# An H3 convolution mixer and a token MLP on one core: where ssm_D is added, how the filter is cut, and a new order of the work

## The chip, the core and the metric

The kernel runs on one core of one Trainium2 chip. A core has five engines with a queue of instructions each: TensorE (PE, matmuls into PSUM), VectorE (DVE), ScalarE (ACT), GpSimd (POOL) and SyncE (SP, which here only starts DMAs). Every engine works through its queue in order and waits on semaphores. DMAs started by SP, ACT or POOL move data between HBM and SBUF, and also between partitions of SBUF. The metric is the device time of one execution in microseconds, the median of the runs shown.

## The reference

With S = 2048 positions, D = 448 channels and F = 1792:

```python
k_shift = sum over t of k_pad[:, t:t+S, :] * shift_k[:, ks-1-t]      # 4 taps
kv      = k_shift * v
y       = irfft(rfft(kv, 2S) * rfft(ssm_k, 2S))[:S]                  # causal convolution per channel
y       = y + kv * ssm_D
h       = x + layernorm(x) * y                                       # x is A_q
# token MLP on the normalised h, along S:
u  = gelu(einsum("bsd,sf->bdf", layernorm(layernorm(h)), w1) + b1)
h2 = h + transpose(einsum("bdf,fs->bds", u, w2) + b2)
```

The kernel computes h as x + (x - mean) * rstd * y. Since y + kv * D is a convolution with a filter whose tap at position 0 has D added, ssm_D can be put into the filter: in the frequency domain it is one constant added to the real parts of the filter's spectrum.

## The kernel before, in words

S is split as 2048 = 128 partitions x 16 rows (r). The convolution is a Fourier transform of length 4096 in two stages of matmuls against sine tables, for the filter k and for the signal u = kv:

- **Loads** (L855 to L880). SP loads the filter ssm_k (448 x 2048) in chunks of 128, 128, 128 and 64 channels, the taps, k, v, ssm_D and the biases.
- **Tables** (L740 to L840). POOL makes indices, DVE phases and ACT sines, in two halves; table E serves the first stage, FW the second, ET (E transposed by PE, the `ct` step, L1035) the last inverse stage.
- **kT** (L962). PE transposes the filter into KT, 64 transposes into eight PSUM banks; ACT or DVE copies each out (the helper `evac`, L698 to L705). Matmuls of constants (L952) lie in between; nobody reads their result.
- **kv** (L915 to L935). Four matmuls with a column of ones spread the four tap rows over 128 partitions. Then DVE multiplies k by the taps (L926), PE sums the four products with the identity as weights (L932), and DVE multiplies the sum by v out of PSUM (L935), in eight steps.
- **First forward stage** of k and of u (`emit_stage1`, L985): for each of four groups i and four jh, eight matmuls of 128 x 32 weights, an evacuation of 896 columns (L997), and, after every second one, a shuffle between partitions by three DMAs (L1002; two from POOL, one from SP).
- **Second forward stage** (`k2` and `u2`, L1021): 16 evacuations each.
- **Products and first inverse stage** (`i1`): DVE multiplies the two spectra (L1054, 16 times), PE transforms (L1066), ACT or DVE evacuates 16 times, and DMAs shuffle the result to TZ (L1090, the last ones L1079).
- **Second inverse stage** (`i2`, L1157): two matmuls per row r; ACT or DVE multiplies by rstd of x and adds 1 (L1164, L1166); DVE multiplies with x - mean (L1171) and normalises over D (L1177 to L1212), POOL making the powers -0.5 (L1130 for x, L1206 for h). The statistics of x come from DVE (L1122, L1124) and POOL (L1127). Matmuls that nobody reads (L1100, "warm") fill PE until the shuffle has landed and between the first rows.
- **MLP**: first layer (L1257 and L1267, 14 groups of 16 accumulating matmuls), gelu on ACT (L1247), second layer (L1277, 16 rows of 14 matmuls), bias and h added by DVE (L1281), output by SP.

No loop in the program sets the order. Each step is recorded as an operation with its reads and writes; `_Sched.schedule` then plays the whole list with estimated costs (`est`) and lets each free engine take the ready operation with the smallest due number. Those numbers are the table `WHEN`, one per step; `WHERE` says for each evacuation that may go to either engine whether it goes to ACT ("a"), to DVE ("d") or to whichever is free ("f"). The order so planned is emitted as the queues, with waits on semaphores where an operation needs another engine's result. So a change of these two tables moves work on all five queues. PSUM holds four pairs of banks, the shuffle ring four groups.

ssm_D enters in the first forward stage of k: for the matmuls of row r = 0 a second matmul with one row of weights (L990, K = 1) adds DR to the sum in PSUM:

```python
dl = tag == "k" and r == 0
op("pe", ... E[:, 2 * r + x, c0:c0 + 32], src[:, r, :], start=True, stop=not dl ...)
if dl:
    op("pe", ... E[0:1, x, c0:c0 + 32], DR[0:1, :], start=False, stop=True ...)
```

Of the kernel before, what the change touches and what calls it, by code (L numbers as in the profile page):

```python
# [7 lines left out]
ALU = mybir.AluOpType  # L8
# [4 lines left out]
    "dummy": (60,),  # L13
    "tables": (47, 16, 57, 90, 51, 55, 62, 200,),
    "loads": (107, 109, 110, 113, 92, 114, 181, 186, 182, 117, 183, 180, 112,),
    "kv": (0, 152, 118, 19, 40, 142, 157, 143, 161,),
    "kT": (189, 78, 21, 33, 268, 73, 150, 8, 160, 83, 132, 72, 108, 122, 100, 95, 70, 53, 129, 46, 91, 115, 65, 48,
        41, 99, 97, 15, 240, 22, 185, 77, 23, 88, 52, 131, 18, 106, 199, 4,),
    "k1": (98, 104, 145, 140, 32, 76, 124, 154, 79, 1, 134, 159, 102, 141, 147, 156,),
    "k2": (166, 165, 120, 105, 168, 167, 146, 148, 170, 169, 178, 176, 171, 172, 184, 179,),  # L20
    "u1": (28, 38, 82, 162, 39, 96, 119, 144, 11, 26, 43, 128, 5, 49, 66, 138,),
    "xload": (6, 264, 256, 195,),
    "ct": (269,),
    "bias": (29,),
    "q": (273, 271, 272, 263, 260, 262, 275, 266, 265,),
    "u2": (69, 68, 17, 10, 103, 116, 50, 42, 121, 123, 80, 126, 125, 151, 133, 127,),
    "i1": (270, 163, 139, 149, 71, 155, 9, 137, 158, 174, 12, 94, 173, 27, 136, 135,),
    "w1a": (67, 75, 85, 87,),
    "w1b": (35,),
    "warm": (64, 56, 254, 274, 250, 247, 255, 130, 81, 164, 30, 252, 241, 20, 249, 235, 7, 37, 25, 89, 101, 251, 267,  # L30
        93, 257, 259, 253, 258, 208, 246, 86, 111, 276, 177,),
    "i2": (61, 13, 14, 175, 44, 45, 34, 187, 192, 3, 31, 188, 204, 245, 63, 203, 243, 194, 244, 205, 74, 190, 24, 84,
        237, 2, 193, 36, 54, 196, 191,),
    "w2": (153,),
    "mlp": (238, 216, 207, 242, 215, 261, 219, 222, 232, 210, 236, 59, 230, 211, 202, 198, 212, 206, 197, 224, 209,
        221, 218, 220, 214, 201, 233, 231, 226, 225, 217, 223, 227, 239, 228, 234, 213, 58, 229, 248,),
}
WHERE = {
    "kv": "fffa",
    "kT": "fdffdffd",  # L40
    "k2": "ddadfafaaddafffa",
    "ct": "ddaa",
    "bias": "f",
    "u2": "afffffaaafaaafdf",
    "i1": "dadffaaffaafafda",
    "i2": "aaaadffaaffadaff",
# [69 lines left out]
class _Buf:  # L116
    __slots__ = ("pool", "k", "users", "writers", "readers", "slots", "left", "rel")

    def __init__(self, pool, k=1):
        self.pool = pool  # L120
        self.k = k
        self.users = []
        self.writers = []
        self.readers = []
        self.slots = None
        self.left = 0
        self.rel = 0.0


class _Op:  # L130
    __slots__ = ("id", "engs", "eng", "fn", "preds", "spreds", "est", "lat", "is_dma", "nbytes", "keng", "ev",
                 "t0", "rate", "acq", "bufs", "tag", "extra")


class _Sched:
# [51 lines left out]
    def op(self, W, fn, r=(), w=(), br=(), bw=(), n=0, kind=None, est=None, dmab=None, keng=16, rate=None, after=(), safter=()):  # L187
# [3 lines left out]
        o = _Op()  # L191
# [14 lines left out]
        o.ev = None  # L206
        o.t0 = WHEN[self.tag][self.count[self.tag]]
# [88 lines left out]
    def schedule(self):  # L296
# [33 lines left out]
        fab = 0.0  # L330
        events = []
# [34 lines left out]
        while done < n:  # L366
            progressed = False
            for e in ENGS:
                if free_at[e] <= t + 1e-9 and ready[e]:
# [21 lines left out]
                    for b in o.acq:  # L391
                        p = b.pool
                        b.slots = pick(p, b.k)
                        for i in b.slots:
                            o.extra.extend(p.prev[i])
                            p.free_t[i] = INF
                    start[cand] = t
                    free_at[e] = t + o.est[e]
                    if o.is_dma:
# [157 lines left out]
def _build(nc, A_q, A_k, A_v, A_shift_k, A_ssm_k, A_ssm_D, B_w1, B_b1, B_w2, B_b2, out):  # L557
# [55 lines left out]
    with ctx:  # L613
# [63 lines left out]
        def Pb(b, i=0):  # L677
            return PS[:, b.slots[i], 0:D]
# [170 lines left out]
        CW = (128, 128, 128, 64)  # L849

# [486 lines left out]
```

## Time and profile before

| | us |
|---|---|
| median of 5 runs | 187.42 (186.85 to 188.64) |
| the profiled execution | 187.61 |
| its span in the profile | 185.7 |
| PE busy | 177.1 |
| PE weight loads busy | 92.9 |
| DVE busy | 109.4 |
| ACT busy | 95.1 |
| POOL busy | 61.5 |

The granted clock of TensorE is 1.0 in the whole span. Busy times are sums over the span, and a matmul's end is modelled, so a busy PE is not one at its peak. Duration and pace differ: instructions that follow one another overlap a little, so five copies listed at 916 ns each can take less than five times that. In lists by group, the columns are line, engine, operation, out<-in, the shape, the count, then busy us and mean ns of one, then the idle time of the engine ahead of them with what ended it. PEld is the loading of weights.

### The profile page before, as it was taken

To read this page: it belongs to the slowest core of one execution; us is meant where nothing else is said; L and a number is where in the kernel's file an instruction comes from. 1 tells how busy PE (TensorE), PEld (TensorE's weight loads), DVE (VectorE), ACT (ScalarE), POOL (GpSimd) and SP (SyncE) were. 2 spreads that over 40 slices of the span, in tenths; PEclk is the share of its full clock that TensorE was granted. 3 is DMA by queue.
4 is the path that set the end of the run, shared out by engine and by line. 5 is a ranking of instruction groups with operands and counts; after the bars stand their busy time and mean duration, and the time that the engine had idled before them with its cause. 6 is when DMAs were issued, how large, how long until landed. Compare 5 with 4: busy or idle time off the path is not lost.

```text
span 185.7 us, 3193 instructions
## 1 busy us (share of the span) xinstructions
PE 177.1 (95%) x1231; PEld 92.9 (50%) x1231; DVE 109.4 (59%) x182; ACT 95.1 (51%) x138; POOL 61.5 (33%) x153
## 2 busy tenths in 40 slices
PE   7999999999888899999999899999999999999993
PEld 2475333333232333544544344556555577777772
DVE  7968788985779999979998674100000034312221
ACT  3577988896999999951785464412222200000000
POOL 8541519556410055358588764000000000000000
DMA  4999626649649957758999999200000002110022
GB/s 120 408 382 352 219 85 240 231 186 315 223 117 340 399 159 202 215 191 264 397 404 407 422 423 415 110 0 4 0 0 0 0 4 99 49 49 25 0 102 74
DMA packets 14869, 35.44 MB, mean 191 GB/s; under 512 B 3133, under 2 KB 8782, under 8 KB 14854
## 3 DMA queue, kind: packets, MB, share of 16 engines
q1 hardware_dynamic: 11734, 28.41, 41.1%
q0 software_dynamic: 3072, 6.80, 11.6%
q8 instruction: 10, 0.16, 0.4%
q14 instruction: 5, 0.04, 0.1%
q10 hardware_dynamic: 48, 0.03, 0.1%
HBM read 22.37 MB, written 1.84 MB: 130 GB/s over the span
## 4 chain that ended last, share of the span: by engine, by line
PE 83%; ACT 11%; POOL 3%; issue 1%; DVE 1%
PE ps L1277 23%; PE ps L1267 11%; PE ps L1257 8%; PE ps L932 7%; PE ps L985 7%; PE ps L1066 6%; PE ps L1100 5%; ACT arena L701 5%; PE ps L962 3%; PE ps L1157 3%; PE ps L952 3%; ACT arena L997 3%; ACT arena L702 3%; PE ps L1021 2%; PE ps L1035 1%
## 5 line engine op out<-in xcount | busy, mean ns | idle before, releaser
L1281 DVE SCALAR_TENSOR_TENSOR arena<-ps,arena 128x448 bf16<-128x448 f32 x16 | 10.9, 684 | 55.9 <-PE ps L1277 55.9
L1277 PE MATMUL ps<-arena 128*128 128x448 bf16 x224 | 43.8, 353 | 0.0
L1277 PEld LDWEIGHTS ps<-arena 128*128 128x128 bf16 x224 | 32.0, 144 | 11.0 <-ACT arena L1247 1.2
L997 ACT CAST arena<-ps 128x896 bf16<-128x896 f32 x32 | 27.2, 916 | 6.1 <-PE ps L985 6.0
L701 ACT CAST arena<-ps 128x896 bf16<-128x896 f32 (+2 forms) x30 | 23.2, 845 | 5.3 <-PE ps L915 2.8
L1257 PE MATMUL ps<-arena 128*128 128x448 bf16 x112 | 24.4, 353 | 0.4 <-DVE arena L1212 0.4
L1002 POOL DMA_DIRECT2D arena<-arena x32 | 17.7, 558 | 20.4 <-ACT arena L997 20.4
L1267 PE MATMUL ps<-arena 128*128 128x448 bf16 x112 | 22.7, 352 | 0.0
L1247 ACT ACTIVATE arena<-ps,arena 128x448 bf16<-128x448 f32 x14 | 8.5, 634 | 25.1 <-PE ps L1267 21.1
L926 DVE TENSOR_TENSOR arena<-arena 128x1792 bf16<-128x1792 bf16 x16 | 17.1, 1101 | 2.2 <-PE ps L932 2.2
L985 PE MATMUL ps<-arena 128*32 128x448 bf16 x256 | 17.0, 356 | 0.8 <-ACT arena L997 0.4
L1021 PE MATMUL ps<-arena 128*64 128x448 bf16 x128 | 15.8, 361 | 2.0 <-ACT arena L701 1.1
L1054 DVE TENSOR_TENSOR arena<-arena 128x1792 bf16<-128x1792 bf16 x16 | 16.7, 1086 | 0.2
L1257 PEld LDWEIGHTS ps<-arena 128*128 128x128 bf16 x112 | 10.8, 98 | 11.3 <-DVE arena L1212 1.8
L1267 PEld LDWEIGHTS ps<-arena 128*128 128x128 bf16 x112 | 10.9, 98 | 9.9 <-ACT arena L1247 0.2
L1164 ACT ACTIVATE arena<-ps,arena 128x448 f32<-128x448 f32 x14 | 9.8, 722 | 11.1 <-PE ps L1157 7.3
L1090 POOL DMA_DIRECT2D arena<-arena x14 | 8.2, 589 | 20.2 <-ACT arena L701 18.1
L1066 PE MATMUL ps<-arena 64*128 64x448 bf16 x128 | 14.1, 351 | 0.6 <-ACT arena L701 0.5
L932 PE MATMUL ps<-arena 128*128 128x448 bf16 x64 | 14.0, 354 | 0.0
L1171 DVE SCALAR_TENSOR_TENSOR arena<-arena 128x448 f32<-128x448 bf16 x16 | 10.7, 677 | 1.6 <-ACT arena L1164 1.6
L1021 PEld LDWEIGHTS ps<-arena 128*64 128x64 f16 x128 | 5.3, 108 | 12.1 <-ACT arena L701 4.7
L985 PEld LDWEIGHTS ps<-arena 128*32 128x32 f16 x256 | 5.5, 95 | 10.0 <-issue 3.3
(87 smaller groups left out, 196.8 us busy)
## 6 DMA issues: line engine op xcount, KB each, us to landing
arena<-in_B_w_dram SPq DMA_DIRECT2D x8, 896.0 KB, 8.5
arena<-in_B_w_dram SPq DMA_DIRECT2D x2, 2048.0 KB, 16.2
arena<-arena SPq DMA_DIRECT2D x16, 224.0 KB, 2.7
arena<-arena POOLq DMA_DIRECT2D x32, 112.0 KB, 2.9
arena<-in_B_w_dram SPq DMA_DIRECT2D x2, 1536.0 KB, 20.9
arena<-arena POOLq DMA_DIRECT2D x14, 196.0 KB, 4.4
arena<-in_A_k_dram SPq DMA_DIRECT2D x4, 448.0 KB, 7.3
arena<-in_A_v_dram SPq DMA_DIRECT2D x4, 448.0 KB, 8.0
```

Of the source, the lines that this page charges most:

```text
L701: return e.copy(out=dst(), in_=src())
L926: op("dve", lambda e, W, T=T, i=i, r=r: e.tensor_tensor(out=T[:, i], in0=KH[:, r:r + 4, :], in1=WT, op=ALU.mult), r=[(o_KH + r * DB, 4 * D ...
L932: op("pe", lambda e, W, b=b, T=T, i=i, j=j: e.matmul(Pb(b, i), ID, T[:, i, j, :], start=(j == 0), stop=(j == 3)), r=[(o_ID, 256), (o + (i ...
L985: op("pe", lambda e, W, b=b, r=r, q=q, x=x, c0=c0, dl=dl: e.matmul(PS[32 * q:32 * q + 32, b.slots[x], 0:D], E[:, 2 * r + x, c0:c0 + 32], s ...
L997: return e.copy(out=dst, in_=Ppair(b)) if W == "act" else e.tensor_copy(out=dst, in_=Ppair(b))
L1002: shuf[tag].append(op(q_, lambda e, W, g=g, i=i, a=a, nu=nu, jh=jh: e.dma_start(T[a + i:a + i + 4 * nu - 3:4].rearrange("p (j k) c d -> p ...
L1021: op("pe", lambda e, W, b=bs[h], h=h, j=j, c=c, par=par: e.matmul(PS[64 * par:64 * par + 64, b.slots[c], 0:D], FW[:, 64 * c:64 * c + 64], ...
L1054: op("dve", lambda e, W, m=m, i=i: e.tensor_tensor(out=MR(m.slots[0]).rearrange("p (x y) d -> p x y d", x=2), in0=TU[:, i].unsqueeze(2).br ...
L1066: k = op("pe", lambda e, W, b=bs[h], m=ms[h], par=par, t=t, tab=tab, xy=xy, P=P: e.matmul(Pb(b, par), tab[P, :], MR(m.slots[0])[P, xy, :], ...
L1257: op("pe", lambda e, W, r=r, fc=fc, b=bs[fc]: e.matmul(Pb(b), W1A[:, r, 128 * fc:128 * fc + 128], Q[:, r, :], start=(r == 0), stop=(r == R ...
L1267: op("pe", lambda e, W, r=r, fc=fc, b=b: e.matmul(Pb(b), W1B[:, r, 128 * (fc - n0):128 * (fc - n0) + 128], Q[:, r, :], start=(r == 0), sto ...
L1277: op("pe", lambda e, W, r=r, fc=fc, b=b: e.matmul(Pb(b), W2[fc // 7][:, fc % 7, r:S:R], G[:, fc, :], start=(fc == 0), stop=(fc == NFC - 1) ...
```

## The change

It has five parts.

1. ssm_D is no longer added by L990. DR holds it on 16 partitions, with the other partitions zeroed by POOL, and the four evacuations of k's first group (i = 0) become additions of DR on DVE. The other first-stage evacuations, which only ACT did, may go to ACT or DVE.
2. The filter is loaded and transposed in four chunks of 112 channels.
3. The tap rows are spread by matmuls over all 128 partitions (ONE and SK whole), for which DVE zeroes SK before the load of the taps.
4. `WHEN` and `WHERE` are new throughout, so the order on every queue is.
5. The planner's costs change: 100 ns when PE changes the shape of its tiles (`mode`), other estimates for some POOL and PE operations. Every operation on a buffer, not only the first, now waits for the readers of the buffer's previous owner.

The numbers of the lines in the changed kernel are some 8 to 10 higher.

```diff
@@ planner
                         for i in b.slots:
-                            o.extra.extend(p.prev[i])
+                            b.extra.extend(p.prev[i])
                             p.free_t[i] = INF
+                    for b in o.bufs:
+                        o.extra.extend(b.extra)
                     start[cand] = t
                     free_at[e] = t + o.est[e]
+                    if e == "pe":
+                        free_at[e] += 100.0 * (o.mode != mode)
+                        mode = o.mode
@@ loads
-                op(Dq, lambda e, W, c=c: e.dma_start(KN[0:CW[c], c, :], A_ssm_k[128 * c:128 * c + CW[c], :]),
-                   w=[(o_KN + 4096 * c, 4096)], dmab=CW[c] * 4096)
+                op(Dq, lambda e, W, c=c: e.dma_start(KN[0:112, c, :], A_ssm_k[112 * c:112 * c + 112, :]),
+                   w=[(o_KN + 4096 * c, 4096)], dmab=112 * 4096)
             sch.t0 = -15.0
+            op("dve", lambda e, W: e.memset(SK, 0.0), w=[(o_SK, 3584)], est=600.0)
...
-            op(Dq, lambda e, W: e.dma_start(DR[0:1, :], A_ssm_D.rearrange("(a d) -> a d", a=1)), w=[(o_DR, DB)],
-               dmab=DB, keng=1)
+            op("pool", lambda e, W: e.memset(DR, 0.0), w=[(o_DR, DB)], est=400.0)
+            op(Dq, lambda e, W: e.dma_start(DR[0:16, :], A_ssm_D.rearrange("(a d) -> a d", a=1).broadcast_to([16, D])),
+               w=[(o_DR, DB)], dmab=16 * DB)
@@ kv
-                    Pb(b), ONE[0:1, :], SK[0:1, :].rearrange("p (d j) -> p j d", j=4)[:, 3 - j, :], start=True, stop=True),
-                   r=[(o_one, 256), (o_SK, 3584)], bw=[b], n=D, est=480.0)
+                    Pb(b), ONE, SK.rearrange("p (d j) -> p j d", j=4)[:, 3 - j, :], start=True, stop=True),
+                   r=[(o_one, 256), (o_SK, 3584)], bw=[b], n=D)
@@ first forward stage
-                            if dl:
-                                op("pe", lambda e, W, b=b, x=x, c0=c0: e.matmul(
-                                    PS[0:32, b.slots[x], 0:D], E[0:1, x, c0:c0 + 32], DR[0:1, :], start=False, stop=True,
-                                    tile_position=(0, 0)),
-                                   r=[(o_E + 256 * x + 2 * c0, 64), (o_DR, DB)], bw=[b], n=D, est=290.0)
...
+                        if tag == "k" and i == 0:
+                            return e.tensor_tensor(out=dst, in0=Ppair(b), in1=DR.unsqueeze(1).broadcast_to([128, 2, D]),
+                                                   op=ALU.add)
...
-                    op("act", fn, br=[b], bw=[g], n=2 * D, kind="psum")
+                    first = tag == "k" and i == 0
+                    op("dve" if first else FX, fn, r=[(o_DR, DB)] if first else [], br=[b], bw=[g], n=2 * D, kind="psum")
@@ the tables (one step of each shown)
-    "u1": (28, 38, 82, 162, 39, 96, 119, 144, 11, 26, 43, 128, 5, 49, 66, 138,),
+    "u1": (94, 55, 106, 158, 124, 128, 177, 191, 207, 62, 223, 236, 82, 120, 217, 234,),
-    "kT": "fdffdffd",
+    "kT": "afadaafd",
+    "k1": "aaaaffaaaadd",
```

On the queues: PE's changes between tile shapes fall from 63 to 30; the table transposes (`ct`) go from the end of the first inverse stage into the filter's transposes and the first forward stage; k's and u's first-stage groups alternate; all 16 statistics of x and their powers stand ahead of the first normalisation of h.

## The prediction

> **What bounds the kernel now.** I read the page's busy times first, then the chain of waits in order of time, then busy time by stretch, and last the groups of instructions and the timeline, for durations. The page:
>
> ```profile
> PE 177.1 (95%) x1231; PEld 92.9 (50%) x1231; DVE 109.4 (59%) x182; ACT 95.1 (51%) x138; POOL 61.5 (33%) x153
> ```
>
> PE looks full, but that is an average over two halves. The chain (start us, us, what):
>
> ```profile
> 12.62 2.56 PE ps L962 x28
> 15.18 1.05 PE ps L985 x17
> ...
> 55.70 5.83 ACT arena L701 x7
> ...
> 80.58 0.67 PE ps L1066 x5
> 81.66 5.11 PE ps L1100 x27
> 86.76 1.28 PE ps L1157 x6
> ...
> 147.28 35.58 PE ps L1277 x188
> 182.88 0.69 DVE arena L1281
> ```
>
> The 27 matmuls of L1100 are filler that nobody reads: PE runs them while the last convolution result is evacuated and shuffled by DMA. From the first L1157 (second inverse stage; L1165 in the changed kernel, as L1257 is L1265) at 86.7 PE only works off its queue: 32 of L1157, 18 fillers, 448 MLP matmuls, 498 in all. The row of 188 gives 35.58/188 = 0.1893 us each, so 94.3 us; the stretch 86.73 to 182.86 has 96.1, so 1.8 us of it is waiting. The end is therefore set by when the first L1157 starts. Before that, busy time by stretch (end of startup to the last product with v; from there to the last evacuation before L1157):
>
> ```profile
> core 0: us, PE busy (x) PEld busy (x) DVE busy (x) ACT busy (x) POOL busy (x), PEclk, DMA share, GB/s
> 15.10:45.60 30.50, 30.03 (x306) 11.42 (x304) 25.87 (x27) 25.33 (x31) 16.71 (x30) 1.00 0.63 223
> 45.60:82.40 36.80, 33.88 (x324) 13.28 (x321) 32.84 (x36) 34.38 (x42) 11.99 (x21) 1.00 0.73 235
> ```
>
> In the first PE is as good as full; in the second ACT (93%) and DVE (89%), which copy every PSUM result out, are the tight pair. The change acts there.
>
> **Durations.**
>
> ```profile
> L997 ACT CAST arena<-ps 128x896 bf16<-128x896 f32 x32 | 27.2, 916 | 6.1 <-PE ps L985 6.0
> L926 DVE TENSOR_TENSOR arena<-arena 128x1792 bf16<-128x1792 bf16 x16 | 17.1, 1101 | 2.2 <-PE ps L932 2.2
> L935 DVE TENSOR_TENSOR arena<-ps,arena 128x896 bf16<-128x896 f32 x8 | 8.7, 1085 | 2.3 <-PE ps L932 2.3
> L990 PE MATMUL ps<-arena 1*32 1x448 bf16 x8 | 2.9, 358 | 0.0
> L944 DVE MEMSET arena<- 128x448 bf16 x1 | 0.4, 432 | 0.9 <-PEq L1322 0.9
> ```
>
> Instructions in a row overlap by some 80 ns, so I count by pace: five L997 in 4.23 us are 0.84 each on ACT, two L926 in 2.08 are 1.03 on DVE, and a PSUM pass on DVE takes 1.0.
>
> **ssm_D.** The eight K=1 matmuls of L990 go. In the timeline the next L985 starts 0.29 us after each, so PE loses 8 x 0.29 = 2.3 us of work in the stretch where it is full. In their place the four evacuations of k's first group go from ACT (4 x 0.84 = 3.4) to DVE as adds from PSUM and SBUF. No such add with a repeated row is in the trace; L935 has its shape and operands, L704, the plain copy, has 1087 ns: both ends are 1.0, so 4.0 us on DVE. The row of D now goes to 16 partitions behind a POOL memset of 128x448. POOL's 128x128 memset takes 0.20 and its 1x1344 one 1.21: between 0.5 and 1.2 us, at about 6 us, where POOL's new order has nothing else until the first shuffles, at 17 before. SP reaches that load at 7.4 us, after the memset, with v's third load and the last loads of k and v behind it; the adds come 20 us later.
>
> **112-row chunks.** 64 transposes remain 64 (0.09 us each, set by the weight load at 0.1); 1.8 MB remain 1.8 MB. All four loads now stand in SP's first five places, and the two bias loads behind them: the last chunk is issued about 0.8 us earlier. PE isn't waiting on loads after 9.8 us, so this gives nothing.
>
> **Tap rows.** Four matmuls of L915 took 1.67 us at K=1. With K=128 they cost 0.19 to 0.37 each (a filler before and after the clock rose): 0 to 0.9 us less. They need SK zeroed, a DVE memset that now stands ahead of everything on DVE: L944 pays 0.43 for 448 elements, so 0.86 for 896. Behind it wait the fillers' own memset, the identity and the sine arguments, and SP's third load until about 1.8 us, which SP reaches at 1.7. So PE starts 0.86 later.
>
> **Start, in the new order.** PE begins at 2.2; nine fillers at 0.396 end at 5.8; up to the transposes that DVE's last filter evacuation needs stand 38 transposes (3.4), nine fillers (2.8) and the taps (1.3): 13.3. The evacuation ends at 14.1 and DVE begins the products with the taps, which it did at 15.8 before: five of the eight filter evacuations are ACT's now, one was.
>
> **To the last product with v.** DVE has 16 x 1.03 + 8 x 1.0 + 4 x 1.0 + 1.5 (small table pieces) = 30.0, to 44.1. Waits: 0.6 where L945 stands behind two products and PE's sums, and some 0.6 behind ACT, which runs the second half of its sines (2.0 us) only after its first k evacuation. So 45.3, against 45.6. PE, full before, has the 2.3 us less, but 16 of 32 table transposes (1.0) more; its changes of tile shape over the whole order fall from 63 to 30 and cost about 0.11 each (eight L932 behind L985 take 1.62, not 1.51). The second forward stage's first matmuls now stand on PE ahead of five v groups and wait for k's shuffles; k's last evacuation of them is at about 41, issue (0.56) and landing (2.9) make 44.5, and PE is there at 46. Each user of a buffer now waits for its previous owners; on one engine that is the order anyway, and only the four groups that ACT and DVE fill together gain a wait, for shuffles that landed long before.
>
> **To the last evacuation.** DVE: 2 + 7 + 4 + 1 = 14 passes, 16 products, three statistics (1.8): 32.3. ACT: 5 + 9 + 12 + 15 = 41 passes, 34.4 from 46.1. The four table evacuations (2.0 on ACT, 1.4 on DVE) have left this stretch. DVE's sum ends at 77.6; behind its last product come eight matmuls and an ACT pass, 1.9: 79.5. ACT's own ends at 80.5. I add 1.5 us of waits to DVE's, since the last two products stand behind ACT's last k passes: 81.0, against 82.37. Gain 1.4.
>
> **To the first L1157.** 4.36 us before: two POOL issues at 0.59 and 2.9 of landing. The new order puts a POOL power (0.71) between the shuffle issues, but in the gap of one ACT pass (0.84): nothing; without that gap 0.7.
>
> **The rest.** 497 matmuls instead of 498: -0.2. All 16 row statistics (0.55 + 0.10) and eight power pairs (0.95) now stand before the first normalisation. DVE has 8.8 us of them after its last product, so its first combine comes 6.9 us after the last evacuation instead of 5.7, and the first MLP matmul, for which PE has 31 x 0.19 = 5.9 us of cover, waits about 1.2. In return the waits at 99.4 and 104.1 (0.4, 0.5), which came from exactly these pieces in between, go. I take 1.5 of waits for 1.8. Stage: -0.5. Tail unchanged.
>
> Sum: 1.4 + 0.5 = 1.9 off the profiled execution's 187.61 (span 185.7), 185.7; that execution lay 0.2 above the median 187.42, so **185.5**.
>
> **A rule against the change.** By my walk PE has about 2.5 us without work from 20.6 (both product pairs read, the next ones still on DVE); before, no single wait of PE was over 1.0 us after the start, and fillers ran at 0.19 from 11.5 on. The Trainium skill, "TensorE: Matmul & The Clock Gate", section "What's actually happening", has the array fall to half clock after about 3.4 us idle. By the row nothing is lost; by the rule, if that gap grew by a microsecond, matmuls would take 0.375 as at the start until such a window of work has passed, 1.7 us more on PE. DVE sets the pace there, so I put in nothing and keep up to 1.7 for the range.
>
> **Rivals.**
> (a) Slower: DVE becomes the bound of the front half. From 14.1 to the last evacuation it carries 62.3 us of work where it carried 57 (four adds, six k passes in stage 1 instead of none); I allow 2.7 of waits where the trace of before has 8.6 in the two stretches. Each further microsecond moves the end by one. From 4.1 on nothing is gained; at 7 the last evacuation is at 85.3 and the time 189.8. For it: waits of 2.3 on L932's sums and 2.2 on L926's buffers. Against: half of before's waits were slack of a less loaded DVE.
> (b) Better: the order takes all waits out of that half (last evacuation 79.5, as DVE's sum has it) and the later ones too (0.5 left): 183.0. For it: the table work is gone from the tight stretch and its shape changes are halved.
> (c) The gain is made and given back: statistics and powers hold the first MLP matmul for 2.5 us instead of 1.2: 186.8, no change.
>
> **Chances.** Forecast with its near values (184.4 to 186.4) 0.40, (b) 0.22, (c) 0.17, (a) 0.21. Within 1% (185.55 to 189.29, about what a measurement of this kernel can tell from no change) lie half of the forecast's and (c). Faster 0.42, same 0.37, slower 0.21. Likeliest range 184.4 to 186.4; for 8 in 10, 183.0 to 189.6.
>
> **What would show it.** Right: the k adds at 1.0 to 1.1 us on DVE; first product with the taps near 14; last product with v near 45.3; last evacuation before the z shuffle on ACT near 81; first L1165 near 85.3; a wait of about 1 us at the first L1265 and almost none after. Wrong: DVE idle over 4 us before the last evacuation, fillers or sums at 0.375 after 20 us, or the first L1165 later than 86.7.

## The result, and the profile after

The changed kernel takes 186.54 us (median of 28 runs, 184.84 to 187.75), the kernel before 187.64 (47 runs, 186.47 to 188.64): a ratio of 0.9942, 95% interval 0.9926 to 0.9959, so 1.1 us faster (0.8 to 1.4). The forecast was 185.5: the direction is right, and a little over half of the 1.9 us came.

The profiled execution of the changed kernel took 187.61 us (span 185.8), 1.1 more than its own median, whereas that of before lies at its median. This page must therefore be read as one of the longer executions. Its busy times:

```profile
PE 171.4 (92%) x1223; PEld 91.3 (49%) x1223; DVE 111.6 (60%) x184; ACT 94.7 (51%) x137; POOL 63.9 (34%) x154
```

PE has 5.7 us less to do than before, the other engines nearly the same. The chain of waits, in order of time (start us, us, what):

```profile
5.38 9.85 DMA arena<-in_B_b_dram
15.23 0.05 issue
15.27 0.18 PE ps L911
...
51.74 5.00 DMA arena<-arena
56.74 0.04 issue
56.78 0.96 PE ps L1029 x8
...
77.28 1.10 DVE arena L1062
78.38 0.05 issue
78.43 0.97 PE ps L1074 x8
79.41 0.05 issue
79.45 0.74 PE ps L1108 x3
80.19 0.86 PE ps L1074 x8
...
81.96 0.91 ACT arena L711
82.88 0.29 issue
83.16 0.63 POOL arena L1087
83.80 3.46 DMA arena<-arena
87.26 0.05 issue
87.31 0.57 PE ps L1165 x2
```

The chain of before has no DMA in it. Here three stand in it: the load of a bias, which PE's transpose L911 waited for; a shuffle at 51.7 that took 5.0 us to land (the median of these shuffles is 3.0); and the last shuffle. The first L1165 is at 87.3, where before had its first L1157 at 86.7. From there to the end PE has 95.6 us, 96.1 before. Busy time in the two stretches, cut at the first product with the taps, the last product with v and the last evacuation (the first cut of before lay at PE's first L985, 0.7 us ahead of its first product; from that product on its shares are the same):

```profile
core 0: us, PE busy (x) PEld busy (x) DVE busy (x) ACT busy (x) POOL busy (x), PEclk, DMA share, GB/s
13.30:44.60 31.30, 28.48 (x319) 12.64 (x319) 29.66 (x36) 27.91 (x33) 18.73 (x32) 1.00 0.70 254
44.60:82.90 38.30, 33.97 (x324) 12.52 (x319) 35.84 (x47) 34.64 (x42) 14.09 (x25) 1.00 0.73 230
```

In the first stretch DVE is now at 95%, where it had 85%, and PE fell from 98% to 91%: DVE took PE's place as the busiest engine there. Durations, by group and shape:

```profile
L936 DVE TENSOR_TENSOR arena<-arena 128x1792 bf16<-128x1792 bf16 x16 | 17.2, 1101 | 0.7 <-DMA arena<-in_A_k_dram 0.7
L945 DVE TENSOR_TENSOR arena<-ps,arena 128x896 bf16<-128x896 f32 x8 | 8.7, 1086 | 0.9 <-PE ps L942 0.8
L1002 DVE TENSOR_TENSOR arena<-ps,arena 128x896 bf16<-128x896 f32 x4 | 4.3, 1084 | 0.0
L866 DVE MEMSET arena<- 128x896 uint32 x1 | 0.8, 805 | 1.0 <-PEq L1330 1.0
```

The new adds of ssm_D (L1002) cost what L945 costs, as forecast, and the memset took 0.81 (0.86 forecast).

### The profile page after: what moved, and what is told of

Same layout as the page of the kernel before. It is cut to its first block, busy times and chain, and to the rows that moved or that the text cites. A ratio compares the mean times of both kernels' runs of the same rounds, so it can differ in the third digit from the quotient of the medians.

```text
span 185.8 us, 3172 instructions
## 1 busy us (share of the span) xinstructions
PE 171.4 (92%) x1223; PEld 91.3 (49%) x1223; DVE 111.6 (60%) x184; ACT 94.7 (51%) x137; POOL 63.9 (34%) x154
## 4 chain that ended last, share of the span: by engine, by line
PE 57%; ACT 13%; DMA 11%; DVE 8%; POOL 5%; issue 2%; SPq 2%; POOLq 0%
PE ps L1285 23%; PE ps L1275 11%; PE ps L1265 11%; DMA arena<-arena 6%; DMA arena<-in_B_b_dram 5%; ACT arena L711 5%; PE ps L1074 4%; ACT arena L1004 4%; POOL arena L1010 3%; DVE arena L936 3%; ACT arena L712 2%; PE ps L1165 2%; DVE arena L945 2%; PE ps L942 2%; PE ps L1029 2%
## 5 line engine op out<-in xcount | busy, mean ns | idle before, releaser
L1285 PE MATMUL ps<-arena 128*128 128x448 bf16 x224 | 42.8, 353 | 0.0
L711 ACT CAST arena<-ps 128x896 bf16<-128x896 f32 (+1 forms) x30 | 24.4, 887 | 8.2 <-PE ps L925 5.9
L1265 PE MATMUL ps<-arena 128*128 128x448 bf16 x112 | 24.5, 353 | 0.9 <-DVE arena L1220 0.9
L1004 ACT CAST arena<-ps 128x896 bf16<-128x896 f32 x26 | 22.3, 916 | 4.0 <-PE ps L994 3.9
L1275 PE MATMUL ps<-arena 128*128 128x448 bf16 x112 | 22.7, 353 | 0.0
L1029 PE MATMUL ps<-arena 128*64 128x448 bf16 x128 | 15.2, 360 | 3.0 <-DMA arena<-arena 1.5
L994 PE MATMUL ps<-arena 128*32 128x448 bf16 x256 | 15.4, 356 | 1.2 <-ACT arena L1004 0.7
L1265 PEld LDWEIGHTS ps<-arena 128*128 128x128 bf16 x112 | 10.7, 98 | 11.6 <-DVE arena L1220 2.3
L1275 PEld LDWEIGHTS ps<-arena 128*128 128x128 bf16 x112 | 10.7, 98 | 10.6 <-ACT arena L1255 1.3
L1074 PE MATMUL ps<-arena 64*128 64x448 bf16 x128 | 13.9, 352 | 1.3 <-DVE arena L1062 0.5
L942 PE MATMUL ps<-arena 128*128 128x448 bf16 x64 | 13.3, 353 | 0.5 <-DVE arena L945 0.4
L1029 PEld LDWEIGHTS ps<-arena 128*64 128x64 f16 x128 | 5.5, 108 | 12.5 <-ACT arena L711 3.4
L1179 DVE SCALAR_TENSOR_TENSOR arena<-arena 128x448 f32<-128x448 bf16 x16 | 10.6, 674 | 1.2 <-ACT arena L1172 1.2
L1220 DVE TENSOR_SCALAR arena<-arena 128x448 bf16<-128x448 f32 x16 | 7.8, 509 | 5.6 <-POOL arena L1214 5.6
```

The costliest lines, as they stand in the source:

```text
L711: return e.copy(out=dst(), in_=src())
L942: op("pe", lambda e, W, b=b, T=T, i=i, j=j: e.matmul(Pb(b, i), ID, T[:, i, j, :], start=(j == 0), stop=(j == 3)), r=[(o_ID, 256), (o + (i ...
L994: op("pe", lambda e, W, b=b, r=r, q=q, x=x, c0=c0: e.matmul(PS[32 * q:32 * q + 32, b.slots[x], 0:D], E[:, 2 * r + x, c0:c0 + 32], src[:, r ...
L1004: return e.copy(out=dst, in_=Ppair(b)) if W == "act" else e.tensor_copy(out=dst, in_=Ppair(b))
L1029: op("pe", lambda e, W, b=bs[h], h=h, j=j, c=c, par=par: e.matmul(PS[64 * par:64 * par + 64, b.slots[c], 0:D], FW[:, 64 * c:64 * c + 64], ...
L1074: k = op("pe", lambda e, W, b=bs[h], m=ms[h], par=par, t=t, tab=tab, xy=xy, P=P: e.matmul(Pb(b, par), tab[P, :], MR(m.slots[0])[P, xy, :], ...
```

## The experiments

All keep the planned order of the kernel that they are made from; the edit is laid on the queues. Line numbers differ from run to run. Ratios are to the kernel before; the time is (ratio - 1) x the median of before beside which it ran.

| run | ratio | 95% interval | us |
|---|---|---|---|
| the change | 0.9942 | 0.9926 to 0.9959 | -1.1 |
| e1, before without L990 | 0.9937 | 0.9913 to 0.9961 | -1.2 |
| e2, before, ssm_D on DVE | 1.0097 | 1.0064 to 1.0130 | +1.8 |
| e3, before, all three shapes | 1.0017 | 0.9990 to 1.0043 | +0.3 |
| e4, changed, L990 back | 1.0063 | 1.0036 to 1.0091 | +1.2 |
| e5, before, tap rows | 0.9956 | 0.9931 to 0.9981 | -0.8 |
| e6, before, chunks | 0.9968 | 0.9937 to 0.9999 | -0.6 |
| e7, before, tap rows and chunks | 0.9904 | 0.9866 to 0.9942 | -1.8 |
| e8, changed, tap rows with K=1 | 0.9963 | 0.9931 to 0.9995 | -0.7 |
| e9, changed, ACT's DMAs later | 0.9903 | 0.9867 to 0.9939 | -1.8 |
| e10, changed, k groups early | 1.0111 | 1.0067 to 1.0155 | +2.1 |
| e11, changed, three edits | 1.0035 | 0.9993 to 1.0077 | +0.7 |
| e12, e7 with ssm_D in the filter | 0.9868 | 0.9827 to 0.9909 | -2.5 |

### Parts of the change in the old order, and one taken out of the new

**e1**: the K=1 matmuls left out of before.

```diff
-                            if dl:
-                                op("pe", ... E[0:1, x, c0:c0 + 32], DR[0:1, :] ...)
+                            # no ssm_D
```

> The kernel before with its own order; only the eight K=1 matmuls of L990 are left out, and nothing takes their place, so ssm_D is not added. Theory A (what the prediction's sum for ssm_D says: PE is as good as full up to 45.6 us, so work taken from PE there moves the end): up to 2.3 us faster, ratio near 0.988. Theory B (the gain of the changed kernel comes from its new order and the engines that evacuate, not from PE's lighter load): PE's spare time turns into waits for VectorE and ScalarE, and the time is within 0.6 us of before, ratio 0.997 to 1.0.

Measured: -1.2 us, between the two. Busy time in the first stretch of that run, from its first product with the taps (here and in e2 and e4 the columns are those of the table above):

```profile
15.70:44.20 28.50, 26.45 (x288) 10.05 (x280) 25.71 (x27) 24.91 (x31) 17.08 (x30) 1.00 0.66 237
```

PE's share fell from 98% to 93%: of the 2.3 us about half shortens the stretch (28.5 us, 29.8 in before from the same point), the rest became waits.

**e2**: ssm_D on DVE, alone.

```diff
-                        op("act", fn, br=[b], bw=[g], ...)          # k's first group
+                        op("dve", add DR to Ppair(b), ...)
-                            if dl: op("pe", ... DR[0:1, :] ...)
+            op("pool", memset(DR, 0)); DR[0:16, :] loaded behind it
```

> The kernel before with its own order and one part of the change alone: ssm_D is added by VectorE at the evacuation of k's first group (four adds, 4.0 us, with ScalarE's four evacuations, 3.4 us, gone), the K=1 matmuls go. Theory A: PE's 2.3 us win, VectorE had slack in the first stage: 1 to 2 us faster, ratio 0.99 to 0.995. Theory B: in an order that was made for the old placing the adds stand in front of products that PE and ScalarE need, and VectorE's 4.0 us cost as much as PE gains: within 0.6 us of before, or up to 2 us slower, ratio 0.997 to 1.01.

Measured: 1.8 us slower, near theory B's bad end. Against e1 the four adds cost 3.0 us of their 4.0. The same stretch of that run:

```profile
16.60:47.80 31.20, 26.85 (x288) 9.83 (x280) 28.86 (x31) 22.13 (x27) 16.82 (x30) 1.00 0.56 197
```

DVE has 28.9 of 31.2 us, PE only 26.9: the bound moved to DVE. This is the mechanism of rival (a) of the prediction, in the order of before.

**e3**: all three changes of shape, order of before.

```diff
+ as e2, and:
-        CW = (128, 128, 128, 64)
+        CW = (112, 112, 112, 112)
-  ONE[0:1, :], SK[0:1, :]     (four matmuls of L915)
+  ONE, SK                      (op("dve", memset(SK, 0)) first; SK's load third on SP)
```

> The kernel before with its own order and all three changes of shape: ssm_D on VectorE, four chunks of 112 channels, tap rows spread by full matmuls behind VectorE's memset of 0.86 us. What is missing of the changed kernel is the new order and the other engines for the evacuations. Theory A: as the changed kernel, 1.1 us faster, ratio 0.994. Theory B: chunks and tap rows give nothing in this order and the memset takes up to 0.9 us: as the kernel with ssm_D alone or up to 1 us above it, ratio 0.998 to 1.015.

Measured: +0.3 us, no change that can be told. Theory A falls, and the number lies in theory B's range. Its distance to the changed kernel, 0.0075, is what the new order (with the evacuations' other engines) gives on top of the shapes: 1.4 us. But e3 is also 1.5 us better than e2, which theory B did not have: chunks and tap rows do give something. That led to e5 to e8.

**e4**: the changed kernel with the K=1 matmuls back.

```diff
-                        if tag == "k" and i == 0: add DR on DVE
+                        copy on DVE; op("pe", ... E[0:1, x, c0:c0 + 32], DR[0:1, :] ...)
```

> The changed kernel with its own order, with ssm_D added again by eight K=1 matmuls on PE, and VectorE's four adds of k's first group turned into plain copies (same count, same 1.0 us each). Theory A: PE's 2.3 us return in a stretch where it is full, and the time goes back to that of before or above it, ratio 1.0 to 1.006. Theory B: VectorE sets the pace there and PE has the 2.3 us to spare: the time stays with the changed kernel, within 0.6 us of it, ratio 0.993 to 0.997.

Measured: +1.2 us to before, so 2.3 above the changed kernel, just what the prediction counted for eight K=1 matmuls. Its first stretch:

```profile
12.90:46.30 33.40, 31.38 (x329) 13.76 (x327) 29.66 (x36) 28.03 (x33) 19.48 (x32) 1.00 0.65 239
```

DVE's 29.66 are those of the changed kernel to the hundredth, PE has 2.9 more, and the stretch is 2.1 longer. So theory B's "PE has 2.3 us to spare" is wrong: in the new order PE's time counts in full, although DVE is the busier engine. e4 keeps everything else of the change, also the four evacuations on DVE, and is slower than before; ssm_D on DVE in the old order (e2) is slower too. The new order with L990 and with these evacuations back on ACT was not run, so what the move to DVE costs in the new order is not known.

### The tap rows and the chunks

In the first microseconds, these kernels differ in when PE's pace doubles. PE's timeline of before (start us, busy us, engine, line, operation, count):

```profile
9.06 0.95 PE L952 MATMUL ps<-arena 128*128 128x448 bf16 x2
9.80 1.68 PE L962 MATMUL ps<-arena 128*128 128x128 bf16 x18
11.32 1.30 PE L952 MATMUL ps<-arena 128*128 128x448 bf16 x6
12.46 2.72 PE L962 MATMUL ps<-arena 128*128 128x128 bf16 x28
15.11 1.12 PE L985 MATMUL ps<-arena 128*32 128x448 bf16 x17
```

and that of e5, where L988 stands for L952, L998 for L962 and L1021 for L985:

```profile
9.26 0.54 PE L988 MATMUL ps<-arena 128*128 128x448 bf16 x2
9.63 1.28 PE L998 MATMUL ps<-arena 128*128 128x128 bf16 x18
10.75 1.30 PE L988 MATMUL ps<-arena 128*128 128x448 bf16 x6
11.89 2.71 PE L998 MATMUL ps<-arena 128*128 128x128 bf16 x28
14.53 1.12 PE L1021 MATMUL ps<-arena 128*32 128x448 bf16 x17
```

From start to start, the two matmuls of 448 columns at 9 us take 0.37 each in before and 0.19 in e5; in before they are at 0.19 only in the six from 11.3 on. Yet e5's PE started 0.9 us later (behind the memset). The tap matmuls themselves are no shorter: four take 1.7 us in both, and in the changed kernel one takes 0.38 (from 9.12 to 9.51 us) right behind matmuls of 448 columns at 0.19. They read every fourth value of SK; whether that is why, no run shows.

**e5**:

```diff
-                    Pb(b), ONE[0:1, :], SK[0:1, :].rearrange(...)
+                    Pb(b), ONE, SK.rearrange(...)
+            op("dve", memset(SK, 0.0))   # first on DVE; SK's load third on SP
```

> The kernel before with its own order; only the four tap matmuls of L915 become full ones (K=128) behind VectorE's memset of SK and SyncE's third load. Theory C (found in the trace of the run with all three shapes: its matmuls of 448 columns fall to 0.19 us from about 7.5 us on, those of before from about 11 us on; the four K=1 matmuls do not count as work for PE's clock): the first matmul starts 0.9 us later, yet PE's first L985 starts 1 to 1.7 us earlier than the 15.1 of before, the time is 1 to 1.7 us less, ratio 0.991 to 0.995. Theory D (the prediction's sum: the tap rows give 0 to 0.9, the memset takes 0.86): 0 to 0.9 us slower, ratio 1.0 to 1.005.

Measured: -0.8 us, the first L985 at 14.5 instead of 15.1. Theory D falls in its sign; theory C has the sign and a little over half of its size.

**e6**:

```diff
-        CW = (128, 128, 128, 64)
+        CW = (112, 112, 112, 112)
```

> The kernel before with its own order; only the four chunks of 112 channels in place of 128, 128, 128, 64. Theory C (in the run with all three shapes the last 28 transposes took 1.93 us, 0.069 each, against 2.56, 0.091, in before, so a transpose of 112x112 is shorter than one of 128x128): PE's first L985 about 0.6 us earlier, ratio 0.996 to 0.998. Theory D (the prediction: 64 transposes stay 64 at 0.09, nothing): ratio 1.0.

Measured: -0.6 us; the interval ends just below 1. PE's timeline of e6:

```profile
12.37 2.07 PE L984 MATMUL ps<-arena 128*128 128x448 bf16 x6
14.27 1.90 PE L994 MATMUL ps<-arena 112*128 112x112 bf16 x28
16.10 1.12 PE L1017 MATMUL ps<-arena 128*32 128x448 bf16 x17
```

From the first of the 28 transposes to the next matmul pass 1.83 us instead of 2.65 (15.11 - 12.46 in before): 0.065 each against 0.095. But theory C's reason, that a transpose of 112x112 is the shorter one, does not hold. Above, 18 transposes of 128x128 in a row take 1.12 us in e5 (9.63 to 10.75), 0.062 each, as short as those of 112. The 28 of before are of two shapes, as its groups between 12.5 and 15.1 us say:

```profile
L962 PE MATMUL ps<-arena 128*128 128x128 bf16 x22 | 2.2, 233 | 0.0
L962 PE MATMUL ps<-arena 64*128 64x64 bf16 x6 | 0.9, 237 | 0.0
```

The six of the 64-channel chunk stand in three pairs between the others. One by one in the trace, the start comes 0.055 to 0.066 us after that of the transpose ahead where the shape stays, 0.157 to 0.161 where it changes, and then once more 0.084 to 0.114. With seven changes (the last to L985) this makes up the 0.8 us. Four equal chunks leave one change. So the gain comes from the changes of tile shape that the uneven last chunk made, not from smaller transposes.

This profiled execution is 1.5 us above its kernel's median, and the six matmuls before the 28 show why: (14.27 - 12.37)/6 = 0.32 each, so PE's pace doubled only at about 13.9. In the four profiles with K=1 tap rows in the order of before (before, e1, e2, e6) it doubles at 10.7, 10.7, 12.6 and 13.9 us; with full tap matmuls, in either order, it has doubled by 8.5 at the latest.

**e7**: e5 and e6 together.

> The kernel before with its own order and with both the tap rows by full matmuls and the chunks of 112, ssm_D left to its eight K=1 matmuls. Theory C: the 1.5 to 2.2 us that these two gave under ssm_D on VectorE come here too: ratio 0.988 to 0.993, faster than the changed kernel, although the order is that of before. Theory D: both give nothing and the memset costs: ratio 1.0 to 1.005.

Measured: -1.8 us (-1.1 to -2.5): theory C. This kernel has the order of before and its K=1 matmuls, and no part of the change but the two small ones, and it lies below the changed kernel (0.9904 against 0.9942; the intervals overlap a little, 0.9926 to 0.9942).

**e8**: the changed kernel with `ONE[0:1, :], SK[0:1, :]` in L925.

> The changed kernel with its own order; only its four tap matmuls of L925 have K=1 again (VectorE's memset of SK stays). Theory C: PE's matmuls stay at 0.37 us for longer than 8.3 us as they do now, VectorE's last filter evacuation and its first product with the taps come 1 to 2 us later than 13.3, and the time rises by about as much, ratio 0.999 to 1.004. Theory D: the clock rises when it did, at most 0.9 us are lost, ratio 0.994 to 0.998.

Measured: 0.4 us above the changed kernel, with intervals that overlap widely; not told apart. The ratio lies in theory D's range and outside theory C's. In its profile two matmuls of 448 columns at 6.3 us already take 0.19 each: in the new order eleven of them and fourteen transposes come ahead of the tap rows, and the doubling is over before the K=1 matmuls begin. That fits a gain that depends on where the tap rows stand; the times can't show it.

The mean granted clock of each execution points the same way. In 39 of 94 executions of before it is 0.989 to 0.991, as a single stretch of 3.4 us at half clock would make it (1 - 0.5 x 3.4/186 = 0.991). With K=1 tap rows a mean under 0.995 is seen in e1 too (13 of 17), in e2 (4 of 14), e6 and e8 (3 of 12 each). With full ones it is seen in none of the 28 executions of the changed kernel, in none of the 45 of e3, e5, e7, e9 and e12, and in one of 15 of e4; e10 and e11 have a stall of their own. None of the executions counted here with a mean under 0.995 has a profile, so where the stretch lies is not known; and those of before that have it are no slower than the others.

### The stalls that the profile of the changed kernel shows

**e9**:

```diff
 ACT queue:
-  DMA L1087, evacuation L711, DMA L1087
+  evacuation L711, DMA L1087, DMA L1087
```

> The changed kernel with its own order; only the two DMA issues of L1087 on ScalarE's queue go behind ScalarE's last evacuation, where they stood before. Theory E (the changed kernel's last evacuation is late because a DMA issue of 1.41 us stands ahead of it): the evacuation follows PE's last sum directly, the first matmul of the second inverse stage comes about 0.7 us earlier, ratio 0.990 (the changed kernel: 0.994). Theory F (the issued shuffle lands as much later, and it is among the last needed): no change, ratio 0.993 to 0.996.

In the changed kernel ACT's queue reads so (with the idle time and its releaser at the end):

```profile
80.51 1.41 ACTq L1087 DMA_DIRECT2D arena<-arena  x1
81.96 0.91 ACT L711 CAST arena<-ps 128x896 bf16<-128x896 f32 x1 [1.49 <-PE ps L1108]
```

PE's sum is done at 81.06, and the evacuation starts 0.9 us later, when the issue is through. In e9:

```profile
79.62 0.91 ACT L745 CAST arena<-ps 128x896 bf16<-128x896 f32 x1 [0.65 <-PE ps L1109]
79.63 2.23 ACTq L1122 DMA_DIRECT2D arena<-arena  x2
```

The evacuation starts 0.14 after its sum. But from its end (80.53) to the first matmul of the second inverse stage (85.54) pass 5.0 us; in e8, which has the changed kernel's placing and an execution as short, 4.3 (81.34 to 85.66). The moved issues land later, and 0.1 us are left in the profile. In time e9 is 0.7 below the changed kernel, theory E's ratio to the digit, with intervals that overlap (0.9867 to 0.9939, 0.9926 to 0.9959). So the profile speaks for theory F, the ratio for theory E, and the runs don't settle it.

e9 showed something else. Up to 75 us its queues are those of the changed kernel, and so are those of e10 and e4 up to 14 us, bar the K=1 matmuls. PE's wait for the bias (1.13 in the changed kernel's profile) was 0.78 in e4, 0.85 in e10, and none in e9, which had its first product with the taps at 12.9 and its last with v ended at 43.0, not at 44.6. In e8 it was 0.26. The chain of waits of e8 passes through the same load:

```profile
4.85 8.94 DMA arena<-in_B_b_dram
13.79 0.05 issue
13.83 0.18 PE ps L943
```

There the transpose of the bias starts 1.44 us earlier than in the changed kernel's profile (13.83, 15.27), and what follows on the chain comes that much earlier: a product with v at 19.33 instead of 20.77, the first matmul after the late shuffle at 55.24 instead of 56.78, the second inverse stage at 85.66 instead of 87.31, the end 1.6 us earlier (185.97, 187.61). So the changed kernel has a load on its path whose landing differs from execution to execution, and as far as e8 can stand for it this is why its profile lies above its median. The bias loads moved ahead and nothing else was not run.

**e10**:

```diff
 PE:   ... second stage of k (i=0, 1, 4, 5) ... first stage of k, i=3, jh=2, 3
+PE:   ... first stage of k, i=3, jh=2, 3 ... second stage of k (i=0, 1, 4, 5)
 DVE, POOL, SP: the two evacuations and the three shuffles moved likewise
```

> The changed kernel; only the last two groups of k in the first stage (i=3, jh 2 and 3) stand ahead of the second stage's first matmuls, on PE, on VectorE (their evacuations) and on the queues (their three shuffles), so that nine shuffles no longer bunch at 50 us. Theory E (the waits of 1.5 us on PE and 1.7 us on VectorE at 55.6 come from that bunch, whose last landing took 5.0 us instead of 3.0): they shrink to under 0.5 and the time falls by 1 us or more, ratio 0.985 to 0.990. Theory F (another wait is next: the last group of u, evacuated by ScalarE at 51.5, with 0.6 of issue and 3 of landing is there at 55 anyway): 0 to 0.5 us less, ratio 0.991 to 0.995.

Measured: 2.1 us slower, which neither had. The timeline of PE:

```profile
44.70 0.56 PE L1067 MATMUL ps<-arena 128*32 128x448 bf16 x8 [1.31 <-DVE arena L1077]
46.60 1.35 PE L1103 MATMUL ps<-arena 128*64 128x448 bf16 x8 [1.34 <-DVE arena L1077]
```

With the two groups next to each other, PE waits 1.31 and 1.34 us for DVE's two evacuations. And then the granted clock fell (PEclk, the third number from the end):

```profile
43.60:47.00 3.40, 0.96 (x12) 0.38 (x14) 2.13 (x3) 0.44 (x1) 0.16 (x1) 1.00 0.20 57
47.00:50.50 3.50, 3.50 (x28) 1.12 (x26) 2.09 (x2) 1.55 (x2) 0.92 (x2) 0.51 0.44 131
```

After 3.4 us in which PE was busy for 0.96, it ran about 3.4 us at half clock. Half clock is not the whole loss: by the mean granted clock three of the six executions have such a stretch (median 190.6), the other three have none and still take 188.8 to 189.6. The edit made a stall of its own, worse than the one it was to remove, so the question whether the bunched shuffles cost 1.5 us stays open.

**e11**: e9's and e10's edits, and the bias loads ahead of those of k and v.

> The changed kernel with three places mended together: ScalarE's DMA issues behind its last evacuation, the last k groups early, and the two bias loads ahead of the loads of k and v on SyncE (PE's transpose of the bias waited 1.13 us for it). Theory E (these three stalls are what the prediction's front half missed): 1.5 to 2.5 us below the changed kernel, ratio 0.981 to 0.986. Theory F (VectorE and ScalarE are the bound of that half and each stall freed becomes a wait elsewhere): at most 0.7 us, ratio 0.990 to 0.995.

Measured: +0.7 us, 1.4 below e10. It carries e10's stall too (1.07 us of work in 3.4, then half clock from 45.6), so its time tells nothing on its theories. It has no wait for the bias. Four of its twelve executions read the full clock; they take 187.3 to 188.2, about what before takes beside them (187.96), so even these are not below the changed kernel.

### A version that beats both

**e12**: ssm_D added to lag 0 of the transposed filter, one row on one partition, on top of e7.

```diff
-                            if dl: op("pe", ... E[0:1, x, c0:c0 + 32], DR[0:1, :] ...)
+            op("dve", tensor_tensor(out=KT[0:1, 0, :], in0=KT[0:1, 0, :], in1=DR[0:1, :], op=ALU.add))
+            # behind DVE's last filter evacuation; D's load behind the filter's chunks on SP
```

> The kernel before with its own order, the tap rows by full matmuls and the chunks of 112 as in the run with these two, and ssm_D added to the transposed filter itself: its lag 0 is one row of 448 values on one partition, so one small add on VectorE (0.2 to 0.4 us) takes the place of the eight K=1 matmuls. If PE's load there is worth what the run without these matmuls showed (1.2 us) and the two shape changes what their run showed (1.8 us): about 2.8 us below before, ratio 0.984 to 0.987, the fastest of all. If VectorE's add, which the first matmuls with that row wait for, costs what PE gains: as the run with the two shape changes alone, ratio 0.990.

Measured: 185.17 us, ratio 0.9868, 2.5 us below before (1.7 to 3.3) and clear of the changed kernel's interval. The add in the timelines of DVE and of PE:

```profile
14.38 0.37 DVE L920 TENSOR_TENSOR arena<-arena 1x448 bf16<-1x448 bf16 x1
```

```profile
14.90 1.84 PE L1034 MATMUL ps<-arena 128*32 128x448 bf16 x32 [0.24 <-DVE arena L920]
```

0.37 us on DVE and a wait of 0.24 on PE take the place of 2.3 us of matmuls. For the same sum the changed kernel pays four passes of 1.0 us on DVE, in place of four of 0.84 on ACT. The forecast of 2.8 us held but for 0.3. Against e7 alone the intervals overlap (0.9866 to 0.9942), so what the add in the filter gives on top of e7, 0.7 us, is not shown by itself. The new order with this add was not run.

## Why the prediction was half right

**ssm_D.** "PE loses 8 x 0.29 = 2.3 us": e4 measures 2.3 in the new order. In the old order the same matmuls are worth 1.2 (e1). "4.0 us on DVE": the four adds of L1002 have 1084 ns each, as L945. Right; but DVE became the busiest engine of the first stretch by it, and e2 shows what that costs in an order that isn't made for it.

**Chunks.** "64 transposes remain 64 (0.09 us each, set by the weight load at 0.1) ... so this gives nothing": wrong; e6 gains 0.6 us. The 0.09 is a mean over transposes of two shapes with changes of tile shape between them. Where the shape stays a transpose takes 0.062 at full pace, of 112 channels or of 128, so no weight load of 0.1 sets it. The prediction gives a change of tile shape 0.11 us, and then put those that the last chunk makes at nothing. The 63 changes that it counts in before seem to leave them out: with tiles taken by rows and columns (32, 64 or 128) the trace of before has 72, e6 63, the changed kernel 30.

**Tap rows.** "PE starts 0.86 later" is right (2.32, not 1.38: 0.94), "0 to 0.9 us less" is at its lower end, since a full tap matmul takes about 0.4 too. But the working treated the start as a list of durations. In before's order the K=1 matmuls seem to put off, too, the moment from which a matmul takes half as long, and e5 gains 0.8 us net. In the new order this is not shown (e8).

**Start.** First product with the taps at 14.1 forecast, 13.3 measured: 38 transposes were counted at 0.09, and most of them took 0.062. DVE then waited 0.68 for a load of k. "So this gives nothing" left out who waits for the bias loads that moved back: L911 on PE, between 0 and 1.13 us, and in the changed kernel's profile all that follows.

**To the last product with v.** 45.3 forecast, 44.6 in the profile (43.0 in e9's). A little better than forecast, with one error on each side: shorter transposes, and a wait for the bias that the sum did not have.

**To the last evacuation: the step that failed.** The sum gave 81.0 (a gain of 1.4), the profile has 82.87. DVE's busy time from 44.6 to its last product's end at 79.4 is 32.34 us; the prediction had 32.3. Two terms beside it were too small. "1.5 us of waits": DVE's are 34.8 - 32.3 = 2.5, with 1.70 for the shuffle that took 5.0 us to land. "Behind its last product come eight matmuls and an ACT pass, 1.9": it took 82.87 - 79.38 = 3.5, since in the new order three fillers (0.74) stand on PE ahead of the last sum, and a DMA issue on ACT's queue ahead of the last evacuation (0.9). Both can be read from the order alone; I counted the work that the last result needs and not what stands before it on the same queues. The late bias of this execution is not the reason: in e8, with the same queues, the stretch from the last product with v (43.1) to the last evacuation (81.34) is as long, 38.2 us, and DVE waits 1.80 for the same shuffle. Mending ACT's half gave little in e9's profile, as the issue that was put back landed later; by the times that is open.

**To the first L1165.** 4.36 forecast, 4.44 measured; POOL's power in between cost nothing. Right.

**The rest.** Waits in the last stage are 95.6 - 497 x 0.1893 = 1.5 (forecast 1.5), and the stage takes 95.6 instead of 96.1: the forecast -0.5 to the tenth. But the wait of 1.2 that was forecast at the first L1265, behind a first combine 6.9 us after the last evacuation, did not come. DVE's first L1179 started 5.8 us after it, as in before, and the first L1265 at 93.23 followed PE's work with no wait. The longest wait, 0.89, is the eighth L1265's at 96.42, for DVE's L1220, which waited for a power of POOL (L1214). So this sum was right in size by luck: the wait was another one.

So of the median's 1.1 us, 0.5 is the last stage, and by difference 0.6 is the front, where 1.4 were forecast. That difference is worked out from medians and one profile, not measured by itself; how much of it is the stalls of the last step and how much the bias load was not settled, nor what the bunched shuffles take of it.

**The rule against the change.** The gap of 2.5 us that I saw on PE from 20.6 came out at 0.42: first-stage groups filled it, the longest wait of PE between 17 and 50 us is under 0.5, and the granted clock stayed at 1.0. The rule itself (the Trainium skill, "TensorE: Matmul & The Clock Gate", section "What's actually happening": half clock after about 3.4 us idle) met its case in e10, and with less idle time than it asks for: 3.4 us with 0.96 of work in them were enough. The duration of half clock, about 3.4 us, is near the window that it states.

**The rivals.** (a), DVE as the bound at 189.8: its mechanism came in the old order only (e2); that e2's time is 189.6 is chance, as (a) was worked out for the new one. (b), 183.0, no. (c), 186.8 by statistics at the first MLP matmul, no: that wait did not come, though the time is near.

## What to carry to other kernels

A small edit is worth what the engine that sets the pace has to do at that place: the same eight matmuls less saved 1.2 us in the old order and 2.3 in the new one, and with the four passes moved to DVE the old order lost 1.8, so a move between engines and the order must be judged together. A mean duration from a list can hide changes of shape: before carrying it over, look at one instruction after another. Before moving a sum to another full engine, ask whether it can be done on less data: one row of the filter instead of four passes over a group. And when the end of a stage is added up, read the queues of all engines that its last result passes: the fillers and DMA issues that stand before it count as much as the work itself.

## What the hardware showed that was not expected

- In these kernels' first microseconds, matmuls of 448 columns take 0.37 us and later 0.19, while the column PEclk reads 1.00. The traces explain the column: where they hold a record of the clock it begins, as far as the pace can tell, when the pace doubles (10.7 us in e1, 13.9 in e6); four of the fourteen, that of before among them, hold none, and a stretch without a record is counted as 1.00. So the 1.0 of before's whole span says nothing of its first 10.7 us.
- With K=1 matmuls behind eight full ones the pace doubled at 10.7 to 13.9 us, with full ones in their place by 8.5. That a one-row matmul doesn't count as work is what fits. It was not isolated: transposes stand around these matmuls, and in e5 the clock's record begins at 5.4 us, just ahead of the tap rows, so in that execution they cannot have brought the doubling on.
- A change of tile shape between PE transposes put the next start 0.16 us after the last instead of 0.06; transposes of 112 and 128 channels had the same pace.
- Half clock in mid-kernel followed 3.4 us with 0.96 us of work, and lasted about 3.4 us; in e11 1.07 us of work in 3.4 was too little as well.
- A DMA issue on ACT's queue took 0.68 and 1.41 us in the changed kernel, against 0.54 to 0.63 on POOL's for the same shuffles, and the engine's next instruction stood behind it.
- Nine shuffles issued within 3 us: the last landed after 5.0 us where the median is 3.0. A small bias load behind large ones landed after 9.85 us, and the wait for it differed from run to run between 0 and 1.13 us.
